# Zero products in two early pauses, and products of 64x128 in place of 64x64 for two levels of the first tile

## The chip, the cores and the metric

The kernel runs on one core of a Trainium2 chip. The metric is the device time of one execution in microseconds. An execution taken with the hardware profiler gives the trace. Its span runs from the first to the last instruction and is a little shorter than the execution's own time.

## The reference

A linear attention with decay (RWKV-6), 4 batches x 8 heads, 768 steps, 48 channels per head, is followed by an MLP with exact GELU:

```python
state = np.zeros((B, H, D, D))
for t in range(S):
    cur = np.einsum('bhd,bhe->bhde', u[None] * kt, vt)
    y[:, :, t] = np.einsum('bhd,bhde->bhe', rt, state + cur)
    state = wt[:, :, :, None] * state + np.einsum('bhd,bhe->bhde', kt, vt)
x = y.transpose(0, 2, 1, 3).reshape(B * S, H * D)      # 3072 x 384
out = gelu(x @ w_in) @ w_out                           # 384 -> 2048 -> 384
```

r, k, v, w and u are fp32. The weights w_in and w_out arrive in fp64 and are converted to fp32 by the kernel.

## The kernel before

The tokens are worked in eight tiles of 384 (NX = 8, T = 384). While the MLP of tile x-1 runs, the attention of tile x, and a part of tile x+1, run between its steps. Which step of which part comes next is written out by hand in strings (`PLAN`), one per tile. A letter takes the next step of one stream. Every engine has its instructions in that order.

The attention is done in chunks of 64 steps (C = 64). Two heads lie on the two halves of the 128 partitions (`half[0]`, `half[1]`, index g), with 48 channels padded to 64. Two neighbouring chunks are the index p. Inside a chunk the pairs of steps (row later than column) are cut into levels h = 1, 2, 4, 8, 16, 32: a level holds the pairs whose later step is in the second half and whose earlier step is in the first half of a block of 2h steps. For each level TensorE (PE) multiplies k by r into a tile d in PSUM (`products`, line 590). Then VectorE (DVE) multiplies r and k in place by products of the decays, so that the next level can be multiplied (lines 638 to 650). It has to wait until PE has read r and k. Last, the part of d that belongs to the level is copied into a_sb: by DVE with a mask for h < 16 (line 662), by ScalarE (ACT) for h = 16 and 32, a few rows at a time (line 659).

The first tile is special. Nothing else is there for the engines to do, so its attention is split into two units, unit 0 and unit 1, each with half of the heads (np_ = 1, with NI = 6 pairs of chunks for each half). Their steps alternate by `PLAN[0]`, where "." takes a step of unit 0 and "s" a step of unit 1. Each level of a unit is one burst of 24 products. Each of them has 64 rows, 64 columns of weights and 64 moving columns, and occupies a quarter of the array: g selects the half of its rows, p the half of its columns. In fp32 each product is two instructions and two loads of weights, so that the profile shows x48 for a burst. There are seven bursts per unit, h = 1, the diagonal (`diagonal`, line 605, with r x u in place of r), then h = 2 to 32. In order of time the fourteen are

- unit 0 h = 1 and diagonal, unit 1 h = 1 (at 9.72 us), diagonal (11.63), h = 2 (13.91),
- unit 0 h = 2 (15.92), unit 1 h = 4 (17.32) and h = 8, unit 0 h = 4, unit 1 h = 16 (22.15),
- unit 0 h = 8 (23.71), unit 1 h = 32 (25.11), unit 0 h = 16 (26.70), unit 0 h = 32 (28.81).

Between the last two PE transposes unit 1's k (line 834). After them come the products for the states (line 864), DVE's chain of states (line 880), the products with v (line 906) and with the states (line 953), the copies of the result to xT, and then the MLP. Its first two matrix products are plain for the first tile (`h_plain`, line 1229, and `g_plain`, line 1243). From the second tile on both are done with sums of blocks and fewer products (line 1142).

After each burst of the first tile, except those of h = 1, PE runs two products of zeros (`keep_warm(2)`, line 371: bf16, 128x128 weights, 512 moving columns) whose result nobody reads. Sixteen more stand at the kernel's start and six before the first MLP. The call takes a PSUM bank from a pair, mm0 and mm1, by turns:

```python
def bank(name="o_ps", i=None):
    turn["mm"] = 1 - turn["mm"] if i is None else i
    return ps.tile([128, BANK], F32, name=name, tag=f"mm{turn['mm']}")
```

The outputs of `h_plain` and `g_plain` take their banks by the same turns. From the second tile on the bank is named: the first product of its MLP opens mm1, the second mm0.

The bursts' tiles d come from a pool of three pairs of banks, so that a burst also waits until the one three before it has been copied.

Of the kernel before, what the change touches and what calls it, by code (L numbers as in the profile page):

```python
# [21 lines left out]
C = 64  # L22
# [6 lines left out]
NI = Q * N3  # L29
# [161 lines left out]
def kernel(  # L191
# [25 lines left out]
    nc = tc.nc  # L217
    NX = rkw.shape[0]
    NP = u.shape[1]
    NPART = NP // Q  # L220
# [6 lines left out]
    wide = w_in.dtype != F32  # L227
# [13 lines left out]
    def pair(name):  # L241
        return pools["d"].tile([128, 2, BANK], F32, name=name, tag="d")
# [13 lines left out]
# [3 lines that stand above are left out]
# [3 lines left out]
    half = [slice(0, 64), slice(64, 128)]  # L262
# [97 lines left out]
    two = const.tile([128, 1], F32, name="two")  # L360
# [4 lines left out]
    def keep_warm(n, elsewhere=False):  # L365
        if elsewhere:
            t = pair("warm")[:, 0]
        else:
            t = bank("warm")
        for _ in range(n):  # L370
            nc.tensor.matmul(t, lhsT=zeros[:, 0:128], rhs=zeros, start=True, stop=True)
# [42 lines left out]
    for i, h in enumerate(QUARTERS[:1]):  # L414
        for a in range(3):
            w_q = (3 - a) * C // 4
            z = q_ints[1 if a == 0 else 2]
# [77 lines left out]
    def attention(x, unit):  # L495
# [3 lines left out]
        np_ = len(parts)  # L499
# [4 lines left out]
        r, k, w = (bufs[0 if x == 0 or i == 0 and x % 2 == 0 else 1][:, base + i * n_u:base + (i + 1) * n_u]  # L504
                   for i in range(3))
        rc, kc = (z.rearrange("p (b i c t) -> p b i c t", b=np_, c=2, t=C) for z in (r, k))
# [33 lines left out]
        else:  # L540
# [5 lines left out]
            rucs = [ru.rearrange("p (i c t) -> p i c t", c=2, t=C) for ru in rus]  # L546
# [40 lines left out]
        else:  # L587
            yield

        def products(bs, right, width, rest=False):  # L590
            d = pair("d")
            n = 0
            for b in bs:
                for i in range(NI):
                    for g in range(2):
                        for p in range(2):
                            nc.tensor.matmul(d[half[p], g, n * width:(n + 1) * width],  # L597
                                             lhsT=kc[half[g], b, i, p], rhs=right(half[g], b, i, p),
                                             start=True, stop=True)
                    n += 1  # L600
            if x == 0 and not rest:
                keep_warm(2)
            return d[:, :, 0:n * width]

        def diagonal():
            return [products([b], lambda z, b, i, p: rucs[b][z, i, p], C) for b in range(np_)]

        def copy_diagonal(diag):
            for b in range(np_):
                nc.vector.copy_predicated(out=at[:, :, b * NI:(b + 1) * NI],  # L610
                                          mask=masks[0].unsqueeze(1).unsqueeze(1).to_broadcast([128, 2, NI, C]),
                                          data=diag[b].rearrange("p g (i t) -> p g i t", t=C))

        def halves():

            for h in LEVELS:
                m = C // 2 // h
                if np_ < NPART:

                    d = products(range(np_), lambda z, b, i, p: rc[z, b, i, p], C, h == 1)  # L620
                    d = d.rearrange("p g (n m two j) -> p g n m two j", two=2, j=h, m=m)[:, :, :, :, 1, :]
                else:
                    right = rc.rearrange("p b i c (m two j) -> p b i c m two j", two=2, j=h)[:, :, :, :, :, 1, :]
                    d = products(range(np_), lambda z, b, i, p: right[z, b, i, p], C // 2)
                    d = d.rearrange("p g (n m j) -> p g n m j", j=h, m=m)
                if h == 1:
                    yield
                    diag = diagonal()
                yield

                r2 = r.rearrange("p (n two j) -> p n two j", two=2, j=h)[:, :, 1, :]
                t2 = tot[h].rearrange("p (n two) -> p n two", two=2)[:, :, 0:1].to_broadcast(r2.shape)
                k2 = k.rearrange("p (n two j) -> p n two j", two=2, j=h)[:, :, 0, :]
                tk = tot[h].rearrange("p (n two) -> p n two", two=2)[:, :, 1:2].to_broadcast(k2.shape)
                rk = bass.AP(tensor=r2.tensor, offset=r2.offset, ap=[r2.ap[0], [n_u - h, 2]] + list(r2.ap[1:]))
                tt = bass.AP(tensor=t2.tensor, offset=t2.offset, ap=[t2.ap[0], [1, 2]] + list(t2.ap[1:]))

                def update(z, r2=r2, t2=t2, k2=k2, tk=tk):
                    nc.vector.tensor_mul(*((k2, k2, tk) if z is k else (r2, r2, t2)))

                if x == 0 and m == 1:

                    update(k)
                    last_r.append(lambda: update(r))
                elif x == 0 and h == 1:
                    update(r)
                    yield
                    update(k)
                else:
                    nc.vector.tensor_mul(rk, rk, tt)  # L650
                behind.add((x, 2))
                yield
                ah = at.rearrange("p g n (m two j) -> p g n m two j", two=2, j=h)[:, :, :, :, 1, :]
                if h >= 16:

                    for p in range(2):
                        for i in range(m):
                            s = slice(p * 64 + i * 2 * h, p * 64 + i * 2 * h + h)
                            nc.scalar.copy(out=ah[s, :, :, i], in_=d[s, :, :, i])
                else:  # L660
                    mask = masks[h].rearrange("p (m j) -> p m j", j=h).unsqueeze(1).unsqueeze(1)
                    nc.vector.copy_predicated(out=ah, mask=mask.to_broadcast(ah.shape), data=d)
                if h == 1:
                    copy_diagonal(diag)
                yield
# [157 lines left out]

        last_r = []
        yield from halves() if x < 2 else quarters()


# [26 lines left out]
        def vs(b, i, g):  # L854
            o = ((parts[b] * NI + i) * 2 + g) * D
            return loaded[x][1][:, o:o + G]

        kvs = []
        for b in range(np_):
            kv_ps = pair("kv_ps")  # L860
            for i in range(NI):
                for p in range(2):
                    for g in range(2):
                        nc.tensor.matmul(kv_ps[half[g], p, i * D:(i + 1) * D], lhsT=k_t(b, i, p, g),  # L864
                                         rhs=vs(b, i, g)[half[p], 0:D], start=True, stop=True)
# [77 lines left out]
        for i in range(NI):  # L943
            for p in range(2):
                for b in range(np_):
                    q, c3 = divmod(i, N3)
                    for g in range(2):
                        c = 2 * c3 + (p + g) % 2
                        src, c0 = (st, c - 1) if c else (before, NC - 1)
                        if src is None:  # L950
# [3 lines left out]
                                         lhsT=src[half[g], o:o + G], rhs=rc[half[g], b, i, c % 2],  # L954
                                         start=False, stop=True, skip_group_check=True)
        assert x < 2 or h_is_done(x - 1)
        if split:
            for c, copy in enumerate((nc.scalar.copy, nc.vector.tensor_copy)):
                for z in range(2):
                    s = slice(z * G, z * G + D)  # L960
                    copy(out=xT[s, 0:Q, :].rearrange("p q (i c t) -> p (q i) c t", c=2, t=C)[:, :, c, :],
                         in_=ys[0][0][c][s, 0:NI * C].rearrange("p (i t) -> p i t", t=C))
# [3 lines left out]
        for b in reversed(range(np_)):  # L966
            for q in reversed(range(Q)):
# [5 lines left out]
                if which < NJ:  # L973
                    for z in range(2):
                        s = slice(z * G, z * G + D)
# [344 lines left out]


    units = [attention(0, unit) for unit in range(units_of(0))]
    second = load_second(nc.sync)

# [23 lines left out]
    for x in range(NX):  # L1348
        following = attention(x + 1, 0) if x + 1 < NX else iter(())
        if x == 0:  # L1350
            streams = {
                ".": units[0], "s": units[1], "f": following, "c": pieces_of_w, "w": next_v(), "x": warm(),
                "l": chain(weight_in(0, True), islice(second, 5), weight_in(1, True), second, weight_in(2, True)),
            }
        else:
            streams = {
                ".": mlp(x - 1), "s": slots, "f": following,
                "l": load(x + 1, nc.sync),
                "x": sums_of_x(x),
                "w": masks_and_sums() if x == 1 else chain(h_sums(1), g_sums()) if x == 2 else iter(()),  # L1360
                "c": pieces_of_w if x == 1 else iter(()),
            }
        for c in PLAN[x]:
            next(streams[c], None)
        for c in ".slxw" if x == 0 else ".slcwx":
            while next(streams[c], streams) is not streams:
                pass
        slots = following
        if x == 1:
            fewer_pairs()  # L1370
# [62 lines left out]
```

## Time and profile before

| | |
|---|---|
| time, median of 3 runs | 570.64 us (566.69, 570.64, 573.06) |
| the profiled execution's own time | 566.87 us |
| its span | 565.1 us |
| granted TensorE clock, mean | 0.997 |
| HBM read, written | 36.24 MB, 4.72 MB |

Engine times are busy times, and shares are of the span. The first tile's attention takes the first 40 us, and the plain MLP of the first tile, with the attention of the second between its steps, lasts to 121 us. The seven other MLPs fill the rest. In the timeline each line has the start and the length in us, the engine, the line, the operation, the tile written and those read, the shape and the count. In brackets stands the idle time before it and what ended it. In the table by stretch the columns are the stretch, its length, the busy time of PE, of the loads of weights (PEld), DVE, ACT and POOL with the number of instructions, the granted clock of TensorE as a share of the full one, the busy share of the DMA engines and GB/s.

### The profile page before, as it was taken

Reading aid. Unit: us, or ns where it says so; the run is one execution under the profiler, and the core shown is the slowest. Engines: PE = TensorE matmul, PEld = TensorE weight load, DVE = VectorE, ACT = ScalarE, POOL = GpSimd, SP = SyncE. Lnnn points to the kernel's source line nnn. Section 1 sums busy time; section 2 is a strip of 40 time slices with the busy share of each in tenths; the row PEclk is TensorE's granted clock in tenths of the full one; section 3 lists DMA queues with packets and bytes.
Section 4 is the critical chain, followed back from the end, with each engine's and each line's share of the span. In section 5 each row is a group of like instructions: output and inputs, shape, how many; then the busy total and the mean of one; then the engine's idle time right before and its main releaser. Section 6 shows DMA issues by size and latency. Waiting matters only on the chain.

```text
span 565.1 us, 17634 instructions
## 1 busy us (share of the span) xinstructions
PE 553.7 (98%) x7449; PEld 497.0 (88%) x7462; DVE 467.2 (83%) x945; ACT 319.7 (57%) x698; POOL 110.2 (19%) x105
## 2 busy tenths in 40 slices
PE   7899999999999999999999999999999999999997
PEld 4676666579989999999999999999999999999997
DVE  7889969999999978998888988899898989831072
ACT  2379988226952477336882378426772478525730
POOL 4100000004500153004410143003410144002610
PEclk9999999999999999999999999999999999999999
DMA  7469742134871556526743575436743447213721
GB/s 266 153 197 386 279 133 101 46 131 57 105 131 55 126 70 88 142 75 143 95 72 100 166 116 73 93 97 136 97 68 106 117 55 96 43 41 57 99 28 43
DMA packets 73279, 63.35 MB, mean 112 GB/s; under 512 B 33008, under 2 KB 58352, under 8 KB 73200
## 3 DMA queue, kind: packets, MB, share of 16 engines
q1 hardware_dynamic: 50112, 45.62, 26.6%
q0 software_dynamic: 22848, 16.52, 22.5%
q8 instruction: 59, 0.97, 0.7%
q14 instruction: 20, 0.16, 0.1%
q10 hardware_dynamic: 240, 0.08, 0.1%
HBM read 36.24 MB, written 4.72 MB: 72 GB/s over the span
## 4 chain that ended last, share of the span: by engine, by line
PE 87%; DMA 5%; ACT 3%; DVE 3%; issue 1%; ACTq 0%; SPq 0%; DVEq 0%; POOLq 0%
PE u_ps L1142 32%; PE h_ps L1142 16%; PE o_ps L1142 13%; PE o_ps L1243 6%; PE h_ps L1229 5%; PE d L736 4%; DMA g<-o_sb 4%; PE d L597 3%; PE kv_ps L864 2%; PE y_ps L906 2%; PE y_ps L953 2%; DMA rkw<-in_rkw_dram 1%; ACT a_sb L752 1%; DVE st L880 1%; PE d L727 1%
## 5 line engine op out<-in xcount | busy, mean ns | idle before, releaser
L1211 POOL DMA_DIRECT2D g<-o_sb x84 | 101.8, 1326 | 419.7 <-ACT o_sb L1205 387.9
L1142 PE MATMUL h_ps<-xT,w_in_sb 128*128 128x192 f32 x392 | 78.0, 329 | 0.0
L1142 PEld LDWEIGHTS h_ps<-xT,w_in_sb 128*128 128x128 f32 x392 | 65.3, 190 | 1.4 <-ACT g L1197 0.2
L1142 PE MATMUL u_ps<-xT,w_in_sb 128*128 128x192 f32 x224 | 44.8, 328 | 0.0
L1142 PE MATMUL u_ps<-w_out_sb,g 128*128 128x192 f32 x224 | 41.2, 328 | 0.0
L1142 PE MATMUL o_ps<-t,g 128*128 128x192 f32 x224 | 41.0, 327 | 0.0
L752 ACT COPY a_sb<-d 32x320 f32<-32x320 f32 (+5 forms) x108 | 39.1, 362 | 2.2 <-PE d L736 0.3
L1215 ACT ACTIVATE g<-g 128x384 f32<-128x384 f32 x70 | 34.7, 517 | 6.3 <-DMA g<-o_sb 4.1
L1142 PEld LDWEIGHTS u_ps<-xT,w_in_sb 128*128 128x128 f32 x224 | 37.5, 190 | 0.5 <-ACT g L1199 0.2
L1142 PEld LDWEIGHTS o_ps<-t,g 128*128 128x128 f32 x224 | 36.9, 190 | 0.3
L1142 PEld LDWEIGHTS u_ps<-w_out_sb,g 128*128 128x128 f32 x224 | 36.9, 190 | 0.3
L1205 ACT ACTIVATE o_sb<-u_ps 128x384 f32<-128x384 f32 x56 | 27.4, 490 | 16.1 <-PE u_ps L1142 12.7
L1229 PE MATMUL h_ps<-xT,w_in_sb 128*128 128x384 f32 x96 | 33.2, 494 | 0.0
L1243 PE MATMUL o_ps<-w_out_sb,g 128*128 128x384 f32 x96 | 31.7, 489 | 0.0
L1142 PE MATMUL u_ps<-w_extra,g 128*128 128x192 f32 x168 | 30.7, 327 | 0.0
L736 PE MATMUL d<-kx,rkw 64*64 64x96 f32 x1152 | 30.3, 247 | 0.1
L880 DVE SCALAR_TENSOR_TENSOR st<-st,tot_sb,kv_ps 128x48 f32<-128x48 f32 x160 | 29.2, 259 | 1.4 <-PE kv_ps L864 1.2
L1298 ACT ACTIVATE o_sb<-u_ps 128x192 f32<-128x192 f32 x21 | 6.9, 330 | 41.4 <-PE u_ps L1142 41.2
L770 DVE COPY_PREDICATED a_sb<-quarter,d 128x480 f32<-128x480 uint8 (+5 forms) x54 | 23.1, 438 | 8.3 <-PE d L736 7.2
L736 PEld LDWEIGHTS d<-kx,rkw 64*64 64x64 f32 x1152 | 25.0, 133 | 5.3 <-issue 2.8
L1177 ACT ACTIVATE u_ps<-h_ps 128x384 f32<-128x384 f32 x21 | 10.0, 476 | 33.9 <-PE h_ps L1142 20.1
L1267 DVE TENSOR_TENSOR g<-g 128x512 f32<-128x512 f32 x42 | 28.5, 682 | 0.8 <-ACT g L1215 0.4
(200 smaller groups left out, 1253.4 us busy)
## 6 DMA issues: line engine op xcount, KB each, us to landing
g<-o_sb POOLq DMA_DIRECT2D x84, 192.0 KB, 3.7
rkw<-in_rkw_dram SPq DMA_DIRECT2D x54, 256.0 KB, 3.5
raw<-in_w_out_dram SPq DMA_DIRECT2D x8, 768.0 KB, 8.5
v_in<-in_v_dram SPq DMA_DIRECT2D x8, 584.0 KB, 4.0
raw<-in_w_in_dram SPq DMA_DIRECT2D x5, 768.0 KB, 10.7
rkw<-kx SPq DMA_DIRECT2D x72, 48.0 KB, 2.1
out_dram<-o_sb SPq DMA_DIRECT2D x17, 192.0 KB, 2.0
rkw<-in_rkw_dram SPq DMA_DIRECT2D x6, 384.0 KB, 6.0
```

The costliest lines, as they stand in the source:

```text
L597: nc.tensor.matmul(d[half[p], g, n * width:(n + 1) * width], lhsT=kc[half[g], b, i, p], rhs=right(half[g], b, i, p), start=True, stop=True)
L736: nc.tensor.matmul(o[half[p], i * 3 * C // 2:(i + 1) * 3 * C // 2], lhsT=kc[half[g], n // NI, n % NI, p], rhs=rx[half[g], 2 * n + p], star ...
L752: nc.scalar.copy(out=at[z, g, first:behind, (a + 1) * h:], in_=d[z, :, :, to] if g == slice(None) else d[z, :, to])
L770: nc.vector.copy_predicated(out=an[:, :, :, :, (a + 1) * h:], mask=mask.to_broadcast(data.shape), data=data)
L880: nc.vector.scalar_tensor_tensor(out=stq[:, q, c], in0=stq[:, q, c - 1] if c else b4[:, q, NC - 1], scalar=totq[:, q, c:c + 1], in1=kvs[q ...
L1142: nc.tensor.matmul(o, lhsT=lhsT, rhs=rhs, start=start, stop=True, skip_group_check=True)
L1205: nc.scalar.activation(out=saved[q, p], in_=held[q, chain_of[q, p]][:, 0:T], func=AF.Copy, scale=scale)
L1211: nc.gpsimd.dma_start(out=g_of(q, m), in_=of_two(saved[q, p]), accum_op=ALU.add)
L1215: nc.scalar.activation(out=g_of(q, m), in_=g_of(q, m), func=AF.Gelu)
L1229: nc.tensor.matmul(h_ps, lhsT=w_in_sb[:, f // FI, j, f % FI * 128:(f % FI + 1) * 128], rhs=xT[:, j, :], start=(j == 0), stop=(j == NJ - 1))
L1243: nc.tensor.matmul(o, lhsT=gs[f // FG][:, f % FG, i * 128:(i + 1) * 128], rhs=w_out_sb[:, f, :], start=(f == 0), stop=(f == NF - 1))
L1267: (nc.vector.tensor_add if op == "+" else nc.vector.tensor_sub)(*(a(i) for i in (z if z != "E0" else "20", x_, y_)))
```

## The change

The number of zero products after a burst is now an argument, `warm`. After unit 0's diagonal burst there are six in place of two, and after unit 1's burst of h = 1 four in place of none. For h = 16 and 32 of the first tile `products` is replaced by `wide`: 12 products a burst, each of 64 rows and 128 columns of weights, that is of both chunks p of k. The 64 moving columns are the second halves of the blocks of r, of both chunks. So d holds also the products of one chunk's k with the other chunk's r, which nobody reads. ACT's copy takes the part with the chunk's own p.

```diff
-        def products(bs, right, width, rest=False):
+        def products(bs, right, width, warm=2):
...
-            if x == 0 and not rest:
-                keep_warm(2)
+            if x == 0 and warm:
+                keep_warm(warm)
             return d[:, :, 0:n * width]
 
+        def wide(m):
+
+            d = pair("d")
+            right = r.rearrange("p (i c m two j) -> p i c m two j", i=NI, c=2, two=2, m=m)
+            for i in range(NI):
+                for g in range(2):
+                    nc.tensor.matmul(d[:, g, i * C:(i + 1) * C], lhsT=k[half[g], i * 2 * C:(i + 1) * 2 * C],
+                                     rhs=right[half[g], i, :, :, 1], start=True, stop=True)
+            keep_warm(2)
+            return d[:, :, 0:NI * C].rearrange("p g (n c m j) -> p g n c m j", n=NI, c=2, m=m)
+
         def diagonal():
-            return [products([b], lambda z, b, i, p: rucs[b][z, i, p], C) for b in range(np_)]
+            return [products([b], lambda z, b, i, p: rucs[b][z, i, p], C, 2 if unit else 6) for b in range(np_)]
...
-                if np_ < NPART:
-
-                    d = products(range(np_), lambda z, b, i, p: rc[z, b, i, p], C, h == 1)
+                if np_ < NPART and h >= 16:
+                    d = wide(m)
+                elif np_ < NPART:
+
+                    d = products(range(np_), lambda z, b, i, p: rc[z, b, i, p], C, 2 if h > 1 else 4 * unit)
...
-                            nc.scalar.copy(out=ah[s, :, :, i], in_=d[s, :, :, i])
+                            nc.scalar.copy(out=ah[s, :, :, i], in_=d[s, :, :, p, i] if x == 0 else d[s, :, :, i])
```

## The prediction

> **What bounds it now.** I read the page first, then the profile by stretches, the timeline of the first 45 us, and the durations of single loads of weights.
>
> ```profile
> PE 553.7 (98%) x7449; PEld 497.0 (88%) x7462; DVE 467.2 (83%) x945; ACT 319.7 (57%) x698; POOL 110.2 (19%) x105
> ...
> PE 87%; DMA 5%; ACT 3%; DVE 3%; issue 1%; ACTq 0%; SPq 0%; DVEq 0%; POOLq 0%
> ```
>
> TensorE (PE) sets the time. The exception is the start, which is all that the change edits. Busy time of PE, its weight loads, DVE, ACT and POOL by stretch, then granted clock and DMA:
>
> ```profile
> 5.04:8.46 3.42, 3.26 (x105) 2.19 (x104) 1.43 (x8) 1.12 (x2) 3.28 (x9) 1.00 0.99 363
> 8.46:11.87 3.41, 1.52 (x64) 1.09 (x67) 3.24 (x9) 1.12 (x2) 0.00 (x0) 1.00 1.03 406
> 11.87:15.28 3.41, 3.08 (x96) 2.46 (x89) 3.30 (x5) 1.35 (x2) 1.44 (x4) 0.50 0.12 41
> 18.69:22.11 3.42, 2.50 (x98) 1.84 (x100) 3.42 (x6) 0.00 (x0) 0.00 (x0) 1.00 0.97 314
> 45.00:120.00 75.00, 75.00 (x973) 47.62 (x966) 68.17 (x119) 52.76 (x75) 0.00 (x0) 1.00 0.47 171
> ```
>
> Three things: from 45 to 120 us PE is never idle, so what the start loses or gains is carried on; a stretch in which PE was 45% busy (1.52 of 3.41) is followed by one of the same length at half clock, while one at 73% (2.50 of 3.42) is not; and DVE is full from 8.5 to 15.3 us. The timeline of the products and of DVE:
>
> ```profile
> 9.72 0.93 PE L597 MATMUL d<-rkw 64*64 64x64 f32 x48 [0.91 <-DMA rkw<-in_rkw_dram]
> 11.63 1.38 PE L597 MATMUL d<-kx,rkw 64*64 64x64 f32 x48 [0.98 <-DVE a_sb L662]
> 13.91 1.54 PE L597 MATMUL d<-rkw 64*64 64x64 f32 x48
> 15.92 0.93 PE L597 MATMUL d<-rkw 64*64 64x64 f32 x48
> 18.31 0.96 DVE L650 TENSOR_TENSOR rkw<-rkw,tot_sb 128x768 f32<-128x768 f32 x1 [0.87 <-PE d L597]
> 22.15 0.93 PE L597 MATMUL d<-rkw 64*64 64x64 f32 x48
> 25.11 1.13 PE L597 MATMUL d<-rkw 64*64 64x64 f32 x48
> 26.70 0.93 PE L597 MATMUL d<-rkw 64*64 64x64 f32 x48
> 27.70 0.96 DVE L650 TENSOR_TENSOR rkw<-rkw,tot_sb 128x768 f32<-128x768 f32 x1 [0.84 <-PE d L597]
> 28.81 0.93 PE L597 MATMUL d<-rkw 64*64 64x64 f32 x48
> ```
>
> The pauses are the 0.91 and 0.98 us of idleness at 9.72 and 11.63. The bursts at 11.63 and 13.91 are the slowed ones. Those at 22.15, 25.11, 26.70 and 28.81 (W1 to W4: unit 1's levels 16 and 32, then unit 0's) are the four that change shape. DVE waits for PE at 18.31 and 27.70, and at 29.79 (1.13 us) after W4.
>
> **The zero products.** Eight are added, four a pause, at 0.22 us each: the timeline has the last six weight loads of the opening zero products in 1.21 us, each 0.1 long, so (1.21-0.1)/5 apart. That is 0.88 us a pause. The two zero products after unit 0's diagonal burst start at 8.22; six end at 9.54, and the next burst cannot start before its DMA, at 9.69. The four after unit 1's level 1 end near 11.3 and the next burst waits for DVE until 11.49. Cost nothing; without that cover the burst at 9.72 may still slip 1.7 us, since DVE first needs it at 12.44. They lift the stretch from 8.46 to 11.87 to 3.28 of 3.41 us busy (1.52 + 8 x 0.22), so the half clock should not come. What that is worth: unit 1's diagonal ends at 12.56, not 13.01, and its level 2 starts when DVE has ended at 13.62, at 13.69 and not 13.91. From start to start a burst with its two zero products takes 1.40 us (15.92 to 17.32): unit 0's level 2 at 15.09, unit 1's level 4 at 16.49. DVE's update of 15.53 ends then, so 16.55; it ends at 17.48, and DVE goes on at 17.54, not 18.31: 0.77 us of the 0.87. Up to W1 everything hangs on that DVE chain.
>
> **The wide bursts.** A 64x64 burst is 12 steps of four tiles side by side, and ends 0.22 us after the last start (one product's duration, 218 ns): (0.93-0.22)/12 = 59 ns a step. What sets a step?
>
> ```profile
> 51.04 1.60 PE L597 MATMUL d<-rkw 64*64 64x32 f32 x96
> 124.19 0.30 PEld L1142 LDWEIGHTS h_ps<-xT,s_more 128*128 128x128 f32 x2
> ```
>
> The first line, of tile 1, has half as many moving columns in 24 steps: (1.60-0.22)/24 = 58 ns, the same. So it is no matter of moving columns; each tile waits for its 64 columns of weights. The second: two loads of 128 columns with nothing before them, 0.19 us each by their group's mean, are 0.11 us apart. Their durations say the same: 0.129 us at least for 64 columns, 0.186 for 128. A wide burst keeps 64 moving columns per product and has two tiles, the halves of the rows, in place of four: again 12 steps, each behind 128 columns. I take 12 x 0.11 + 0.22 = 1.54 us, 0.61 more than now. Bounds: were the columns streamed the only limit (192 in 0.163 us, eight products of line 1142 in 1.30), a step would be 0.054 and the burst 0.87 us, 0.06 less; if the two halves load in turn, 24 x 0.11 + 0.22 = 2.86, 1.93 more. No row shows a 64x128 tile; I take the middle because the halves do load side by side in the 64x64 bursts.
>
> The Trainium skill, "TensorE: Matmul & The Clock Gate", section "LDWEIGHTS (loading the stationary operand)", has a rule that speaks against this change: a load's time goes with its columns, as columns/1.2 ns, whatever the rows, so a load of fewer rows saves nothing. By it a step is 107 ns and the burst 1.50 us; the trace agrees for 64x64 and 128x128, and is silent on 64x128.
>
> **The sum.** W1 starts 0.77 us earlier, at 21.38. The next burst follows at 21.38+1.40+0.61 = 23.39 (now 23.71; it had waited 0.16 for DVE, which is now early). W2 at 24.79 (25.11), end 26.33. W3 at 26.80 (26.70), end 28.34 (27.63): the gap from W2 to W3 was 1.59, since the 25.11 burst has a hole of 0.2, which I don't carry over. DVE's update at 28.40 (27.70), and W4 0.16 us after its end, at 29.52 (28.81), end 31.06. DVE goes on at 31.12, not 29.79: 1.33 us late. In short, 4 x 0.61, less 0.77, 0.16 and 0.19. From there the transposes, DVE's chain of states to 36 us, ACT's copies and conversions and tile 1's u products (ACT, to 42.4) wait for each other until PE's unbroken work begins at 43.02: the 1.33 us are passed on. ACT's copies of rows have the same count and size: no cost. DMAs move with their issuers; none is added.
>
> One more edit hides in the first: the extra call of the zero products takes one more turn of the two banks mm0 and mm1. Later calls alternate alike, until the first tile's last output block, which would then lie in mm1, where tile 1's first product opens its bank. That product starts at 120.99 today, ACT's copy of the block runs from 120.75 to 121.23; waiting for it costs 0.3 us. Sum: +1.6 us, 566.87 to 568.5 on the profiled execution (span 565.1 plus 1.8). That execution lies 3.8 under the median of the runs, 570.64; the four executions shown average 569.3, and I put the forecast there: 570.9.
>
> **Rivals.**
> *Cheap loads* (ends on the other side): the wide burst is bound by moving columns, 0.87 us. For it: half as many instructions for the same products; the hole in W2 might go with them. Against it: the 58 ns at 32 columns. The saving is 4 x 0.06 + 0.77 + 0.16 + 0.19 less 0.3 of the bank: -1.1 us, 568.2. The sign turns where a wide burst is 0.2 us longer than now, at steps of 76 ns.
> *The halves load in turn*: 4 x 1.93 - 1.12 + 0.3 = +6.9 us, 576.2. Against it: rows already load side by side.
> *The clock is lost or kept anyway*: without the 0.77, +2.4 us, 571.7. For it: the half clock hangs on where a stretch of 3.41 us begins; one from 7.00 has 2.34 us busy (69%), near what stayed at full clock. The same page, section "What's actually happening", has this window run free of the kernel's start, which would make the gain come and go between executions; one trace cannot show that.
> *Absorbed*: a later wait for DMA or ACT swallows the shift: 0, 569.3. Against it: no idleness of PE in 45 to 120 us.
>
> **Chances.** Forecast 0.57, cheap loads 0.17, clock 0.12, in turn 0.08, absorbed 0.06. The executions shown spread from 566.69 to 573.06, more than all cases but one. Range: from cheap loads at the low end, 566.7-1.1 = 565.6, to the forecast at the high end, 573.06+1.6, stretched a little towards the loads in turn: 575. About 1%, 5.7 us, is what a measurement can tell from no change. Slower by more: the loads in turn and the odd median, 0.10; faster by more: no case gives it, only the spread, 0.04; within: 0.86.
>
> **What would show it.** Granted clock 1.00 from 11.87 to 15.28 and bursts of 0.93 at 11.63 and 13.7; DVE's wait at 18.31 nearly gone. Wide bursts of 24 products in about 1.5 us; DVE's waits before the two updates after W3 and W4 longer than 0.84 and 1.13. PE's unbroken work from about 44.3. A wait of 0.3 us for ACT's copy before tile 1's first product. I am wrong if wide bursts take 1.1 us or less, or if the clock halves again.

## The result and the profile after

| | before | after |
|---|---|---|
| time, median | 570.30 us (22 runs) | 573.23 us (22 runs, 571.48 to 575.31) |
| ratio, 95% interval | | 1.0047 [1.0026, 1.0068], about +2.7 us |
| the profiled execution's own time | 566.87 us | 573.91 us |
| its span | 565.1 us | 572.1 us |
| granted TensorE clock, mean | 0.997 | 1.0 |

The changed kernel is slower by about half a per cent. The 22 runs of before lie between 566.69 and 574.97 us but for one of 3210.49, which the ratio leaves out. The two profiled executions lie 7.0 us apart, because that of before is one of its fastest; so the landmarks of single profiles below are read as places and mechanisms, and sizes are taken from the timed runs.

The page of the changed kernel: busy time by engine, and the chain that ended last.

```profile
PE 560.7 (98%) x7374; PEld 499.8 (87%) x7374; DVE 467.6 (82%) x945; ACT 319.5 (56%) x698; POOL 109.8 (19%) x105
...
PE 93%; DMA 3%; ACT 2%; issue 1%; DVE 0%; ACTq 0%; POOLq 0%
```

PE sets the time as before. Its share of the chain rose from 87 to 93%, and DVE's fell from 3% to 0: in the start PE has become the last to arrive. Three of the stretches that were shown of before, in the changed kernel (busy time of PE, its loads, DVE, ACT and POOL, then granted clock, DMA share and GB/s):

```profile
8.46:11.87 3.41, 3.41 (x116) 2.24 (x109) 3.24 (x9) 1.12 (x2) 0.00 (x0) 1.00 1.03 410
11.87:15.28 3.41, 3.10 (x100) 1.89 (x99) 3.04 (x5) 0.77 (x1) 1.07 (x3) 1.00 0.09 29
45.00:120.00 75.00, 72.91 (x1047) 46.65 (x1046) 65.67 (x109) 55.47 (x79) 0.00 (x0) 1.00 0.53 189
```

The zero products fill the stretch from 8.46, and the one from 11.87 keeps the full clock. The last line holds what was not foreseen: 2.1 us of PE's 75 are idle, where there were none. Of these, 0.66 are the wait for ACT before tile 1's diagonal, which starts at 47.13; in before the same wait (0.46) lies ahead of 45 us. The timeline of the changed kernel, PE and DVE:

```profile
10.66 0.93 PE L597 MATMUL d<-rkw 64*64 64x64 f32 x48
11.52 1.04 PE L371 MATMUL warm<-zeros 128*128 128x512 bf16 x4
12.49 0.93 PE L597 MATMUL d<-kx,rkw 64*64 64x64 f32 x48
14.10 0.33 PE L597 MATMUL d<-rkw 64*64 64x64 f32 x2
14.58 0.92 PE L597 MATMUL d<-rkw 64*64 64x64 f32 x46 [0.16 <-issue]
17.37 1.23 PE L597 MATMUL d<-rkw 64*64 64x64 f32 x48
22.47 1.83 PE L611 MATMUL d<-rkw 64*128 64x64 f32 x24
26.16 1.56 PE L611 MATMUL d<-rkw 64*128 64x64 f32 x24
28.19 1.55 PE L611 MATMUL d<-rkw 64*128 64x64 f32 x24
30.90 1.56 PE L611 MATMUL d<-rkw 64*128 64x64 f32 x24
```

```profile
18.64 0.96 DVE L663 TENSOR_TENSOR rkw<-rkw,tot_sb 128x768 f32<-128x768 f32 x1 [0.83 <-PE d L597]
29.79 0.96 DVE L663 TENSOR_TENSOR rkw<-rkw,tot_sb 128x768 f32<-128x768 f32 x1 [1.46 <-PE d L611]
32.49 1.05 DVE L652 TENSOR_TENSOR rkw<-rkw,tot_sb 128x384 f32<-128x384 f32 x2 [1.74 <-PE d L611]
```

And in before the update after W4:

```profile
29.79 1.05 DVE L639 TENSOR_TENSOR rkw<-rkw,tot_sb 128x384 f32<-128x384 f32 x2 [1.13 <-PE d L597]
```

Three of the wide bursts take 1.55 to 1.56 us, the first 1.83, and DVE's waits before the updates after W3 and W4 grew from 0.84 to 1.46 and from 1.13 to 1.74: 0.62 and 0.61 each. But the update at 18.31 has not come earlier; it starts at 18.64. Landmarks of the two profiles, worked out from their timelines (us):

| | before | after | difference |
|---|---|---|---|
| first burst starts | 6.65 | 7.70 | +1.05 |
| DVE's update of 18.31 | 18.31 | 18.64 | +0.33 |
| DVE's update after W4 | 29.79 | 32.49 | +2.70 |
| ACT's copy after the states | 35.75 | 39.74 | +3.99 |
| tile 1's diagonal starts | 43.02 | 47.13 | +4.11 |
| 19th product instruction of `h_plain` after that diagonal | 52.58 | 58.18 | +5.60 |
| tile 0's last output product | 120.23 | 126.29 | +6.06 |
| from there to tile 1's first product | 0.76 | 1.05 | +0.29 |
| from there to the end | 444.11 | 444.80 | +0.69 |

So 2.70 us are lost up to the point that the prediction worked out, and 4.35 more behind it, where it had put 0.3. Those stand in three places on PE, in which it stops inside a run of products that wait for nobody:

```profile
39.14 1.49 PE L966 MATMUL y_ps<-rkw,st 64*64 64x64 f32 x48 [1.07 <-issue]
...
42.59 0.53 PE L597 MATMUL d<-rkw 64*64 64x32 f32 x19 [0.75 <-issue]
...
47.13 2.09 PE L597 MATMUL d<-kx,rkw 64*64 64x64 f32 x94 [0.66 <-ACT kx L544]
50.44 0.27 PE L597 MATMUL d<-kx,rkw 64*64 64x64 f32 x2 [1.22 <-issue]
```

"issue" is time in which PE waited for nothing that the profile shows. In the last two lines the diagonal of 96 instructions breaks after the 94th, although all its data are there. Counted by the starts of products beyond their usual pace, the three are 1.23, 0.92 and 1.39 us. The landmarks show the first (the difference grows from 2.70 to 3.99) and the third (from 4.11 to 5.60); of the second only 0.12 is left, since tile 1's diagonal behind it waits for ACT in both kernels (0.46 and 0.66 us). The last 0.69 us of the table are not explained.

**What these pauses are.** All of PE's records were counted from the first (products, loads of weights, waits). In the changed kernel the pauses stand after records 449, 705, 961 (in the bursts at 14.10, 17.37 and 22.47), 1729, 1985, 2241 (the three above) and 3777 (0.37 us at 92.86): differences of 256 or whole multiples of it. In e9 to e12 below, whose records are complete as well, every pause of over 0.4 us up to 60 us in which PE waits for nothing that the profile shows stands at such a count too (705, 961, 1217, 1473, 1729, 1985, 2241). The page names a queue that moves instructions:

```profile
q8 instruction: 58, 0.95, 0.7%
```

That is 58 packets and 0.95 MB, so 16 KB each; PE has 14,900 records, about 58 times 256. 16 KB for 256 instructions is 64 bytes each. The times of these packets in the trace, next to the pauses of the changed kernel (us):

```
packet of q8 starts   PE pauses from   PE goes on   from the packet
12.19                 14.20            14.58        2.39
15.68                 17.84            18.04        2.36
20.73                 22.86            23.09        2.36
36.94                 37.86            39.14        2.20
40.30                 41.62            42.59        2.30
48.15                 49.00            50.44        2.30
```

PE goes on 2.2 to 2.4 us after a packet has started, every time; at the pauses of e9 to e12 it is 2.3 to 2.8 us. Two packets follow each other by 3.24 us at the least in all profiles taken, and by 3.35 in this one. In a dense 64x64 burst PE starts eight records (four products, four loads) in 59 ns, so that 256 of them last 256/8 x 0.059 = 1.9 us: the products use up a block faster than blocks come. A wide burst has four records in 0.111 us, 7.1 us a block, more than the 3.24 between two packets; the pause in W1 ends a block that 64x64 bursts had mostly used up. In the plain MLP two records take 0.32 us, and there is ample time.

### The profile page after: what moved, and what is told of

It is laid out like the page before. It is cut to its first block, busy times and chain, and to the rows that moved or that the text cites. A ratio compares the mean times of both kernels' runs of the same rounds, so it can differ in the third digit from the quotient of the medians.

```text
span 572.1 us, 17470 instructions
## 1 busy us (share of the span) xinstructions
PE 560.7 (98%) x7374; PEld 499.8 (87%) x7374; DVE 467.6 (82%) x945; ACT 319.5 (56%) x698; POOL 109.8 (19%) x105
## 4 chain that ended last, share of the span: by engine, by line
PE 93%; DMA 3%; ACT 2%; issue 1%; DVE 0%; ACTq 0%; POOLq 0%
PE u_ps L1155 33%; PE h_ps L1155 16%; PE o_ps L1155 14%; PE o_ps L1256 6%; PE h_ps L1242 5%; PE d L749 4%; PE d L597 3%; DMA g<-o_sb 3%; PE warm L371 2%; PE kv_ps L877 2%; PE y_ps L919 2%; PE y_ps L966 2%; PE d L611 1%; PE kt_ps L847 0%; PE d L740 0%
## 5 line engine op out<-in xcount | busy, mean ns | idle before, releaser
L1256 PEld LDWEIGHTS o_ps<-w_out_sb,g 128*128 128x128 f32 x96 | 18.0, 190 | 12.6 <-ACT o_sb L1261 0.5
```

The lines of the kernel that those rows point to most:

```text
L1256: nc.tensor.matmul(o, lhsT=gs[f // FG][:, f % FG, i * 128:(i + 1) * 128], rhs=w_out_sb[:, f, :], start=(f == 0), stop=(f == NF - 1))
```

## The experiments

Two theories run through the expectations. Loads (L): the time follows from the length of the bursts, that is, from the columns of weights that each step loads, as predicted. Blocks (B): in the start PE is also held up by the arrival of its instructions, so that their number, and where each 256th falls, has a price of its own. All ratios are to the kernel before on the same chip; its median there was between 568.1 and 570.5 us. A ratio is not the quotient of the two medians, and differences in us are taken from the ratio.

**e1: the wide bursts alone**, with the zero products as before.

```diff
-            return [products([b], lambda z, b, i, p: rucs[b][z, i, p], C, 2 if unit else 6) for b in range(np_)]
+            return [products([b], lambda z, b, i, p: rucs[b][z, i, p], C) for b in range(np_)]
...
-                    d = products(range(np_), lambda z, b, i, p: rc[z, b, i, p], C, 2 if h > 1 else 4 * unit)
+                    d = products(range(np_), lambda z, b, i, p: rc[z, b, i, p], C, 2 if h > 1 else 0)
```

> The wide bursts without the eight zero products and without the extra turn of the banks. Theory L (the weight loads of the wide bursts are the cost: 4 x 0.61 us, less 0.35 that the waits around them give back): +2.1 us over the kernel before, every wide burst near 1.55 us. Theory B (PE fetches its instructions in blocks of 256 and stands still where a block is used up before the next one is there; the 176 instructions fewer move the ends of the blocks into dense bursts): the same and 1 to 2.6 us more, with holes in PE's record at every 256th instruction, in the products with the states at about 38 us and in tile 1's first bursts.

Measured: 570.15 us against 568.54, ratio 1.0015 [0.9989, 1.0041]. From the update of 18.31 (here at 18.02) to that after W4 (31.60) it takes 13.58 us, in before 11.48: +2.10, where the prediction's terms give 2.44 - 0.16 - 0.19 = 2.09. The middle of the ratio's interval is only +0.9, and its end reaches +2.3; the medians differ by 1.6. The gap before tile 1's first product is 0.76, as without an extra turn of the banks.

**e2: the zero products alone**, with 64x64 bursts and the extra turn.

```diff
-                if np_ < NPART and h >= 16:
+                if False:
...
-                            nc.scalar.copy(out=ah[s, :, :, i], in_=d[s, :, :, p, i] if x == 0 else d[s, :, :, i])
+                            nc.scalar.copy(out=ah[s, :, :, i], in_=d[s, :, :, i])
```

> The eight zero products and the extra turn of the banks, with the bursts of 64x64 as before. Theory L and theory B alike: granted clock 1.00 from 10 to 16 us, a gain of 0 to 0.8 us at DVE's update of 18.3 us, a loss of 0.3 us at tile 1's first product: between -0.5 and +0.3 us against before. Sixteen instructions more move the ends of the blocks little, so no new holes. If the zero products themselves cost time: +0.3 to +1 us, PE late for the bursts after the pauses.

Measured: 568.79 us, 0.9991 [0.9961, 1.0020]. The clock stays full, but the update of 18.31 is at 17.99 and still waits 0.60 us for PE, whose bursts at 13.66 and 16.72 were lengthened by a block's end. In e1, which has the full clock without the zero products, it was at 18.02. The gap is 1.05.

**e3: the changed kernel, its blocks moved** by 88 small and six fewer large zero products at the kernel's start.

```diff
-    keep_warm(16)
+    keep_warm(10)
+    pad = ps.tile([128, BANK], F32, name="pad", tag="mm1")
+    for _ in range(88):
+        nc.tensor.matmul(pad[0:32, 0:32], lhsT=zeros[:, 0:32], rhs=zeros[:, 0:32], start=True, stop=True)
```

> The changed kernel with 88 small zero products (176 instructions) at the opening and 6 of its 16 large ones taken out, so that from 31 us on the ends of PE's blocks of 256 instructions fall on the same instructions as in the kernel before. Theory L: as the changed kernel, +2.9 us over before. Theory B: the holes of 1.28 us at 37.9 and of 1.44 us at 49.0 are gone: 1.2 to 2.6 us less than the changed kernel, within 1.5 us of before.

Measured: 571.99 us, 1.0048 [1.0022, 1.0074]. The pauses at 37.9 and 49.0 are gone: from DVE's second chain of states to ACT's copy 1.51 us and not 2.88, from tile 1's diagonal to the 19th instruction behind it 9.52 and not 11.05. A new one of 2.05 us stands at 11.29, in unit 1's first burst, which is cut in two:

```profile
10.94 0.57 PE L600 MATMUL d<-rkw 64*64 64x64 f32 x22
13.39 0.62 PE L600 MATMUL d<-rkw 64*64 64x64 f32 x26 [1.88 <-issue]
```

The pauses moved with the blocks, as B has it, but nothing was gained: what one place gave, another took.

**e4: the kernel before, its blocks moved** by 40 small and three fewer large zero products, and nothing else.

```diff
-    keep_warm(16)
+    keep_warm(13)
+    pad = ps.tile([128, BANK], F32, name="pad", tag="mm1")
+    for _ in range(40):
+        nc.tensor.matmul(pad[0:32, 0:32], lhsT=zeros[:, 0:32], rhs=zeros[:, 0:32], start=True, stop=True)
```

> The kernel before with 40 small zero products (80 instructions) at the opening and 3 of its 16 large ones taken out, so that from 31 us on the ends of the blocks fall as in the changed kernel; nothing else is changed. Theory L: as before, within 0.3 us. Theory B: holes of about 1 us in the products with the states or in tile 1's first bursts, +1 to +2.6 us over before.

Measured: 573.49 us, 1.0080 [1.0046, 1.0113], +4.6 us. All other work is that of before; the first burst starts at 7.01, in before at 6.65. It is more than the whole change costs. A lost clock does not explain it: the three executions with a granted clock of 1.0 took 570.89, 573.47 and 573.80 us. The longest pause of its profile, 2.65 us, stands in the products with the states (at 36.66), and W4 is cut in two by a block's end:

```profile
28.82 0.65 PE L600 MATMUL d<-rkw 64*64 64x64 f32 x26
30.68 0.57 PE L600 MATMUL d<-rkw 64*64 64x64 f32 x22 [1.22 <-issue]
```

**e5: the kernel before, one more profile.**

> The kernel before once more, for a second profile. Theory B: the blocks that PE crosses at 33.5 and 37.2 us had come 2.38 and 2.23 us after their fetch began, which is what a fetch takes elsewhere (2.0 to 2.4 us), so in another execution one or both come too late and leave a hole of 0.5 to 1.3 us; that would be a part of the 7 us by which the executions of before differ. Theory L: the same trace as before but for the stretch of half clock.

Measured: 570.1 us, 3.2 over the execution profiled first. Nearly all of the difference stands in one place. In the first profile the products for the states run through; in this one they stop, and after their 37th product 2.4 us are lost:

```profile
32.81 1.05 PE L864 MATMUL kv_ps<-v_in,kx 64*64 64x48 f32 x47
```

```profile
33.37 0.78 PE L864 MATMUL kv_ps<-v_in,kx 64*64 64x48 f32 x37
36.59 0.37 PE L864 MATMUL kv_ps<-v_in,kx 64*64 64x48 f32 x10 [2.44 <-issue]
```

The packet for this block started at 34.31; in the first profile the one for the same block had started at 31.10, in time. So within one kernel a block comes in time in one execution and too late in another. The executions of before spread from 566.6 to 577.6 us over all batches (but for the one of 3210.49); how much of this is the blocks is not shown. With 192 records less, e1 spreads from 569.1 to 571.4, but the changed kernel from 571.5 to 575.3.

**e6: e1 with the instructions made up** by small zero products, so that number and blocks are as in before.

```diff
-            keep_warm(2)
+            keep_warm(1)
+            t = ps.tile([128, BANK], F32, name="fill", tag=f"mm{turn['mm']}")
+            for z in range(25):
+                o = z % 4 * 32
+                nc.tensor.matmul(t[o:o + 32, 0:32], lhsT=zeros[:, 0:32], rhs=zeros[:, 0:32], start=True, stop=True)
```

> The wide bursts alone, with the instructions that they save put back: behind each of the four, one large zero product and 25 small ones (32 columns, four places in the array) in place of two large ones. No zero products in the pauses, no extra turn. So the ends of the blocks fall as in the kernel before and only the length of the wide bursts is new. Theory L: 4 x 0.61 less 0.35, +2.1 us over before, between 1.5 and 3. Theory B alone (the length is hidden, only the ends of blocks count): within 0.5 us of before.

Measured: 573.29 us against 569.78, 1.0041 [1.0012, 1.0070]: +2.3 us, with bursts of 1.55 to 1.56. The longer loads are 2.09 of it by the prediction's terms. But the small products cost something of their own: from update to update its profile has 32.38 - 18.17 = 14.21 us, 0.63 more than e1's, of which about 0.2 are a block's end at 25.06. So of the 1.4 us between e6 and e1 some 0.4 are not what fewer instructions give back, and the two intervals overlap. Its profiled execution has a pause of 2.78 us in the products for the states (at 36.39), and after it a stretch at half clock, 38.79 to 42.20.

**e7: e1 with each chunk's own r only**, 24 products of 64x128 weights with 32 moving columns in place of 12 with 64, so that each tile is loaded twice as often.

```diff
-                for g in range(2):
...
+                for p in range(2):
+                    for g in range(2):
+                        o = i * C + p * C // 2
+                        nc.tensor.matmul(d[:, g, o:o + C // 2], lhsT=k[half[g], i * 2 * C:(i + 1) * 2 * C],
+                                         rhs=right[half[g], i, p, :, 1], start=True, stop=True)
```

> The wide bursts as 24 products of 64x128 with 32 moving columns each in place of 12 with 64: as many instructions as before, the same moving columns in sum, twice the loads of weights. No zero products in the pauses, no extra turn. Theory L: a burst of 24 x 0.11 + 0.22 = 2.86 us, +7.4 us over before. If a load waits for the product before it in its tile (0.056 + 0.027 a step): 2.2 us a burst, +4.7 us. If moving columns were the limit: 0.9 us a burst, no change.

Measured: 583.29 us, 1.0218 [1.0181, 1.0255], +12.4 us. The moving columns halved and the loads doubled, and a burst takes nearly twice as long:

```profile
22.42 2.87 PE L613 MATMUL d<-rkw 64*128 64x32 f32 x48
30.69 5.33 PE L613 MATMUL d<-rkw 64*128 64x32 f32 x48 [0.35 <-DVE rkw L306]
```

24 x 0.11 + 0.22 = 2.86 at the full clock: the loads set the pace. The last two, at 30.69 and 38.20, run at half clock, which holds from 30.23 to 47.30 us; the 2 x 2.46 us that they lose by it are about what the measured +12.4 has over the +7.4 of L. PE's record is hardly ever idle in this stretch, nor in the one before it (3.26 of 3.41 us from 26.82; busy times by stretch as above):

```profile
30.23:33.64 3.41, 3.06 (x29) 2.95 (x30) 0.41 (x2) 0.78 (x2) 0.00 (x0) 0.50 0.63 201
```

**e8: e2 with the banks turned back.**

```diff
                 keep_warm(warm)
+                if warm == 4:
+                    turn["mm"] = 1 - turn["mm"]
```

> The eight zero products, 64x64 bursts, and the turn of the two banks put back by one more flip. Against the zero products with the turn: 0.3 us less, tile 1's first product 0.76 us after the start of the last product of the first tile's MLP and not 1.05. Against before: -0.3 to -1.1 us if the clock's gain is there in most executions, 0 if only in the profiled one.

Measured: 568.82 us against 569.78, 0.9995 [0.9974, 1.0015]. The gap is 0.76. And here no early burst is lengthened by a block's end, and DVE's update starts at 17.37, without a wait before it, where the prediction had 17.54:

```profile
17.37 0.96 DVE L665 TENSOR_TENSOR rkw<-rkw,tot_sb 128x768 f32<-128x768 f32 x1
```

**e9: e8 with the level of 32 rows in 24 products of 32 columns of weights and 32 moving columns**, which leaves a quarter of the work and the same number of instructions.

```diff
+                            if few:
+                                nc.tensor.matmul(d[p * 64:p * 64 + 32, g, n * width + 32:(n + 1) * width],
+                                                 lhsT=kc[half[g], b, i, p, 0:32], rhs=right(half[g], b, i, p)[:, 32:64],
+                                                 start=True, stop=True)
+                                continue
...
```

> The zero products in the pauses with the turn put back, and for the level of 32 rows the other way round: 24 products of 64x32 with 32 moving columns, which are all that this level needs (unit 1 at 25.1 us, unit 0 at 28.8). Theory L (a burst is 12 steps, each as long as the load of its columns): a step of 32/128 x 0.107 + 0.004 = 0.031 us, the burst 0.59 in place of 0.93 us, 0.3 to 0.7 us less than the zero products with the turn put back. If a step can't be shorter than about 58 ns for another reason: no change. The number of instructions is that of the kernel before plus 16.

Measured: 572.16 us against 570.52, 1.0032 [0.9999, 1.0064]: not faster. The burst is as short as L has it, 0.61 where 0.59 was expected, and a pause stands behind it:

```profile
29.79 0.61 PE L598 MATMUL d<-rkw 64*32 64x32 f32 x48
...
32.35 0.90 PE L884 MATMUL kv_ps<-v_in,kx 64*64 64x48 f32 x43 [1.16 <-issue]
```

Five successive blocks (records 705 to 1729) each end in a pause, of 0.42, 0.72, 0.87, 1.33 and 1.93 us. This is as B has it: shorter bursts use up the instructions earlier, and here they saved nothing.

**e10: e8 with 168 small zero products more**, to bring the blocks' ends to places where PE waits anyway.

```diff
-                keep_warm(warm)
+                keep_warm(1 if small else warm)
+                if small:
+                    t = ps.tile([128, BANK], F32, name="fill", tag=f"mm{turn['mm']}")
+                    for z in range(22):
+                        o = z % 4 * 32
+                        nc.tensor.matmul(t[o:o + 32, 0:32], lhsT=zeros[:, 0:32], rhs=zeros[:, 0:32], start=True, stop=True)
```

> The zero products in the pauses with the turn put back, and behind four of the early bursts (level 2 of both units, 4 and 8 of unit 1) one large and 22 small zero products in place of two large ones: 168 instructions more before 21 us, which move an end of a block out of unit 0's products for the states (at 32 to 34 us) into its products with v behind them. Theory B: no hole in unit 0's products for the states, where the kernel before has one of 2.6 us in one of its two profiles; the median 0.5 to 2 us below before, and the executions closer together. Theory L: as the zero products with the turn put back, or up to 0.4 us slower for the small products.

Measured: 574.90 us, 1.0065 [1.0033, 1.0097]: a miss. The pause in the products for the states is gone, and others of 1.61, 1.54 and 1.85 us stand at 20.09, 28.76 and 38.17. More instructions bring more blocks, and their ends fall elsewhere.

**e11: the changed kernel with the banks turned back** (the two lines of e8).

> The changed kernel with the banks turned back once behind the first unit's second fill, so that tile 1's first product finds the bank it had before. Bank turn (from the prediction): the gap between the last product of tile 0's output and tile 1's first product is 0.76 us again and not 1.05, and the kernel is 0.3 us under the changed one: about 1.004 of the kernel before, +2.3 us. If the turn were not what makes that gap (other late wait), the gap stays at 1.05 and the ratio at 1.0047. Nothing else should move, since no instruction is added or taken away.

Measured: 572.55 us (6 runs) against 568.11, 1.0094 [1.0062, 1.0126]. The gap is 0.76 again, so the turn makes the 0.29 us. The ratio is a miss: before's median is 2.2 us lower here than beside the changed kernel, while the time itself is 0.7 under the changed kernel's. Its profile shows the diagonal of tile 1 broken after the same product as in the changed kernel, with a longer pause:

```profile
45.99 2.09 PE L597 MATMUL d<-kx,rkw 64*64 64x64 f32 x94 [0.50 <-ACT kx L544]
50.25 0.37 PE L597 MATMUL d<-kx,rkw 64*64 64x64 f32 x2 [2.17 <-issue]
```

The instructions up to there are as many in both, so the block's end falls on the same product, and only the time at which the packet came differs (47.80, when the products ran out at 47.87; 48.15 and 49.00 in the changed kernel).

**e12: of the four wide bursts W1 alone**, banks turned back.

```diff
-                if np_ < NPART and h >= 16:
+                if np_ < NPART and h == 16 and unit == 1:
...
```

> The changed kernel with the banks turned back, and with the wide products in the first of the four bursts alone (unit 1, level 16); 48 instructions fewer than with none wide. Loads (each wide burst is 0.6 us longer): that burst's length lies partly in the wait for unit 1's level 16, which had slack; the other three bursts are back at 0.94, so DVE's update behind the last burst comes 1.8 us earlier than in the changed kernel, and the ratio is 0.999 to 1.001. Instruction blocks: 48 instructions fewer are a fifth of a block of 256, so the time is up to 0.6 us under the kernel before (0.998) if no block ends in the products for the states, and up to 2 us over it (1.004) if one does; its profile tells by the holes at every 256th product.

Measured: 568.73 us against 568.11, 1.0012 [0.9998, 1.0025]. The burst takes 1.55, and from the update of 18.31 (here 18.09) to that after W4 (29.83) 11.74 us pass, 0.26 over before: the rest of the 0.61 went into waits that W1 had. A pause of 1.75 us falls at 33.67, in the products with v. No version tried is faster than before beyond its interval.

## Why the prediction was right, point by point

The forecast was +1.6 us and the measured ratio gives +2.7, with +1.5 to +3.9 by its interval: 570.9 against 573.23. About 1.0 of the 2.3 us between these two times is the base, 569.3 in the forecast and 570.30 here. The mechanism that sets the sign, longer bursts through twice the columns of weights, was right. The sum has one gain that did not come in full, and one cost is not in it; how the missing 1.1 us are shared between them is open. With the gain at nothing the sum is +2.4, which is the rival of the clock "kept anyway" and nearer to what was measured than the forecast; the interval holds both.

- **The wide bursts: right.** 1.54 us forecast, 1.55 to 1.56 measured in all twenty bursts of the changed kernel, e1, e3, e6, e11 and e12 that hold no pause; the step is (1.55 - 0.22)/12 = 0.111 us. The rival of cheap loads (0.87) is out, and so is that of halves that load in turn (2.86): W1 to W4 show neither, and e7 shows that 2.86 is what twice the loads cost. With e9 there are three widths: 0.033 us a step for 32 columns, (0.61 - 0.22)/12, 0.059 for 64 and 0.111 for 128. The Trainium skill's "TensorE: Matmul & The Clock Gate", section "LDWEIGHTS (loading the stationary operand)", has a load's time go with its columns, as columns/1.2 ns, whatever the rows. An estimate by it is 107 ns for a step of 128 columns, and the 111 ns measured with 64 rows agree. From the update at 18.31 to that after W4 the terms gave 2.10; the changed kernel's profile has 13.85 - 11.48 = 2.37, of which 0.27 are a block's end in W1 (1.83 against 1.56 us), and e1 has 2.10. In time, e6 has +2.3 with its small products, e1 +0.9.
- **The gain of the zero products, 0.77: mis-sized.** Where nothing disturbs it, the update comes early: in e8 it starts at 17.37, even before the 17.54 of the sum. In the changed kernel's profile it starts at 18.64. There the first burst came 1.05 us later, by no edit: the granted clock is full from 7.20 us on, in before from 5.06, and until then the opening zero products start 0.43 us apart in place of 0.22. The prediction let the burst of 9.72 slip by 1.7 us and put the cost of the zero products at nothing. It slipped by 0.94, but the four zero products behind it then ran to 12.56 while DVE had been ready at 11.67, so that the diagonal started at 12.49 and not at 11.63. Block ends lengthened the bursts at 14.10 and 17.37 by 0.47 and 0.30 us. In the timed runs the zero products alone are worth 0.3 to 0.5 us (1 - 0.9995 and 1 - 0.9991 of 570), with intervals that hold nothing and 0.77 alike. In the batch of e11 and e12, 7 of the 17 executions of before had a granted clock of 0.996 or 0.997, about what one stretch of 3.41 us at half clock takes off; their median is 567.83 us, that of the other ten 568.23. So there such a stretch cost nothing that the time shows, wherever it lay. In the batch of e9 and e10 those with 0.996 or 0.997 are 4.5 us slower than those with 0.999 or more (573.12 and 568.61), which is more than the 1.7 us that such a stretch can take; something else goes with it there.
- **The half clock: right in kind, and not certain in before.** It came in before from 11.89, in e5 from 11.69, in e6 from 11.48, each time behind a stretch with 1.53 to 1.58 us of busy PE. It came in none of the kernels with the zero products at that place, but neither in e1, e4 and e7, which have none more in the pauses: there the stretch holds 2.07 to 2.17 us. In e1 and e7 it lies later (the clock is full from 6.32 and 6.34 on); in e4 it lies as in e6, and the bursts lie otherwise. That is the rival of the clock "kept anyway", which so holds in a part of the executions: of e1's twelve, eleven have a granted clock of 1.0. The same page of the Trainium skill, section "What's actually happening", has the window run free of the kernel's start, and the different starts of these stretches in kernels with the same opening (before, e1, e5, e6, e7) agree.
- **The turn of the banks, 0.3: right.** 0.29 in the changed kernel, e2 and e3, gone in e8 and e11; it is too small to be seen in the times. The profile names the wait; the product at 127.34 starts when ACT's copy of the block has ended, at 126.81 + 0.48:

```profile
126.81 0.48 ACT L1261 COPY o_sb<-o_ps 128x384 f32<-128x384 f32 x1 [4.48 <-PE o_ps L1256]
```

- **"From there ... the 1.33 us are passed on": this step failed.** It took PE's products between 31 and 49 us to keep their pace, and so the later stages to pass on what came in. In the changed kernel's profile 2.70 came in and 6.06 went out. What stood between is the arrival of PE's instructions, which the prediction did not name: three pauses of 3.54 us together, at the ends of blocks of 256, and one of 0.37 at 92.86. That blocks can cost this much is shown by e4, which moves their ends and changes little else, +4.6 us, and by the pauses' places in five kernels.
- **What the blocks do to the change as a whole is only bounded.** 192 records fewer may be a gain (e1 at +0.9 against e6 at +2.3, less what e6's small products cost). e1 and e2 together come to about +0.4 us and the changed kernel to +2.7; each has its own interval, and together they are about as wide as this difference, so it may be noise. If it is real, the place of the blocks' ends in the changed kernel is a likely reason, but e3, made to show it, removed two pauses and got a third, and so doesn't. Open too is what makes a packet late: the first eight of each of the five kernels start 0.2 to 6.2 us after PE has crossed into the block before the one that they bring, and no run here showed why.
- **Absorbed** is out: in the profile more went out than came in, and the time rose.

## What to carry to other kernels

The pace of small products on a divided array is set by the columns of weights that each step loads; fewer, wider products with the same rows pay for every column added, and multiply unread results. Where dense small products use up instructions faster than they arrive, a shorter burst may buy nothing (e9), and the count of instructions is a cost of its own: where a profile holds all of them, count 256 records along the engine and look for pauses marked "issue" there before crediting a saving or blaming an edit. In a stage with such pauses compare medians of many runs, since one profile may differ from the next by more than the edit is worth, and an edit that only moves the blocks can cost as much as a real one.

## What the runs showed that was not expected

- PE's instructions come in blocks of 256 (16 KB). Where it had to wait, PE went on 2.2 to 2.8 us after the block's packet started; packets followed each other by 3.24 us at the least, and a dense 64x64 burst uses a block up in 1.9 us. Moving the blocks' ends alone cost 4.6 us (e4).
- The busy time in PE's record does not by itself tell when the half clock comes. In e7 it came behind a stretch busy for 3.26 of 3.41 us, in before the full clock stayed behind one of 2.50, and a stretch of 1.82 was followed by half clock (e12, from 32.66), one of 1.75 by full (e4, from 11.50). What the clock counts as busy is open.
- Pauses of 1.75 to 2.78 us brought one more stretch of half clock with them in four profiles (e6 at 38.79, e9 at 38.41, e11 at 49.98, e12 at 36.08), so a late block can cost twice; in e4 and e5 pauses as long brought none.
